# Attention and a cosine-gated feed-forward on one core: work moved from VectorE to Pool, a new order in a step, and split copies

## The chip, the cores and the metric

The kernel runs on one core of a Trainium2 chip. A core has a matmul engine (TensorE, PE in the profile), a vector engine (VectorE, DVE), a scalar engine (ScalarE, ACT), a general engine (Pool, POOL) and a queue engine that issues transfers (SyncE, SP). They run side by side and wait for each other by semaphores. Each works through its own instructions in the order in which the program gives them. The metric is the device time of one execution in microseconds (us); lower is better. All times below are from chip runs of the kernel before the change.

## The reference

Eight batches of 512 tokens, eight heads of 64 columns and 32 state rows per head. Tokens read the state and the state reads the tokens (two softmax attentions). The 544 rows of a batch, 512 columns wide, then pass through a feed-forward layer with 2048 hidden columns whose gate is h cos h:

```python
scores = scale * x @ state.T;  a = softmax(scores);   xread = a @ state
scores2 = scale * state @ x.T; a2 = softmax(scores2); sread = a2 @ x
y = concat([xread, sread], axis=2)        # (8, 8, 544, 64)
x = y.transpose(0, 2, 1, 3).reshape(4352, 512)
h = x @ w_in                               # (4352, 2048)
out = (h * cos(h)) @ w_out                 # (4352, 512)
```

x and state are float32. w_in and w_out arrive as float64 and are used as float32.

## The kernel before

**Main loop.** One step of the loop at L746 works one tile of 128 hidden columns. Steps 0 to 127 are the token tiles: batch b = step // 16, tile f = step % 16, 512 tokens wide. Steps 128 to 143 are the state tiles, all 256 state rows at once; their n-th tile has f = (n + 8) % 16. A step makes h (`hidden`, L416) in one of two PSUM buffers, then the gate: ScalarE adds a large constant to round (`gate`, L425), VectorE takes the remainder (`gate2`, L428), ScalarE takes Abs and Sin (`gate3`, L433 and L434), VectorE multiplies by h (`gate4`, L440). The result g goes to one of 28 slots of g_all. The products with w_out (`output`, L555) come three steps later (`LAG`).

**Attention inside h.** h is not made from the attention's output. For each batch the product of the state with w_in is made first (`products`, L389) and copied to the tile sw (`products_kept`, L394); h is sw times the softmax weights aT. The products of batches 0 and 1 use the PSUM banks o1* (SIDE), those of later batches the banks at*.

**The order in a step.** It is written out by hand at L753 to L798. `plan(b)` (L666) gives lists for each step: attention work for TensorE (`go(0)`), for ScalarE after `gate` (`go(1)`) and after `gate3` (`go(2)`), for VectorE after `gate2` (`go(3)`) and after the product (`go(4)`). In `plan`, `early` is the scores and softmax of a batch (tokens are transposed twice, then scores, maximum, spread, exponentials, sums, normalisation) and `late` is the reading of the tokens by the state (two transposes `turn`, two matmul groups `reads`, the scaling `keep`, the transpose `turned`). The last reads of a batch release the loads of the next batch's x on SP's queue.

**Pairs of batches.** Two batches form a pair, and their four half-batches of g (phase 0 to 3, eight tiles each) are multiplied with the quarters of w_out (a11, a12, a21, a22) by a scheme with seven products in place of eight. It needs sums of weight quarters (s1 to s4, `blocks`, L731: eight instructions of 128x1024 at steps 13 to 23) and differences of g (`minus`, L442, called from `sums` and `sums2`: one per step in phase 2, three in phase 3). Two of the products run in the next pair's steps (`more`). When the first product of phase 0 or 2 is complete, `keep_product` (L491) copies both channels of its PSUM bank (MAIN) to a held tile, and only then may TensorE start the next product in that bank.

**Conversion.** A float64 weight becomes float32 in parts (`convert_part`, L198): "1" Abs of the high words and "2" the low words on ScalarE, "a" a maximum, "b" a shift, "c" an xor and "d" a 32-bit integer addition of e on VectorE. Eighteen loads are converted, four of them ahead of the loop and one in each of steps 0 to 13; part d of a load runs in the step after its other parts. s3 overwrites the quarter a21; two more loads (L161) bring it back, and they are converted at steps 136 and 137, with part d one step later. The state tiles need the quarter again from step 139 on.

Of the kernel before, what the change touches and what calls it, by code (L numbers as in the profile page):

```python
# [23 lines left out]
def kernel(  # L24
# [164 lines left out]
    def convert(i, parts):  # L189


        if i < len(loads) and f64:
            for p in parts:
                convert_part(i, p)
        if "c" in parts and i + 3 < N_LOADS:
            fetch(i + 4)

    def convert_part(i, p):  # L198
# [15 lines left out]
        elif p == "c":  # L214
            nc.vector.scalar_tensor_tensor(out=bits, in0=raw[:, :, :, 1],
                                           scalar=-2 ** 31, in1=bits,
                                           op0=ALU.bitwise_and,
                                           op1=ALU.bitwise_xor)
        else:
            nc.vector.tensor_tensor(bits, bits, e.bitcast(I32), op=ALU.add)  # L220
# [6 lines left out]
    class Attention:  # L227
# [166 lines left out]
        def products_kept(self, nt, bank=None, c0=0, c1=WC):  # L394
# [47 lines left out]
    def minus(out, a, b):  # L442
        nc.vector.tensor_tensor(out, a, b, op=ALU.subtract)  # L443
# [47 lines left out]
    def keep_product(out, bank):  # L491
        for ch in range(2):
            nc.scalar.activation(out.t[:, ch], acc[bank][ch], func=ACTF.Copy,  # L493
                                 scale=TWO_PI)
# [26 lines left out]
    def sums(t):  # L521
        pr, i = t.pair, t.i
        pr.b[t.phase, i] = t
        if t.phase == 2:
            minus(pr.b[0, i].g, t.g, pr.b[0, i].g)
        if t.phase == 3:
            minus(pr.b[0, i].g, t.g, pr.b[0, i].g)
            minus(pr.b[2, i].g, t.g, pr.b[2, i].g)

    def sums2(t):  # L530
        pr, i = t.pair, t.i
        if t.phase == 3:
            minus(pr.b[1, i].g, pr.b[1, i].g, pr.b[0, i].g)
# [132 lines left out]
    def plan(b):  # L666
# [38 lines left out]
        if b == 0:  # L705
# [23 lines left out]
    conv_at.update({B * NF + 8: N_LOADS, B * NF + 9: N_LOADS + 1})  # L729

    def blocks(op, out_, a, b, r):  # L731
        nc.vector.tensor_tensor(out_[:, r], a[:, r], b[:, r], op=op)
# [13 lines left out]
    for step, t in enumerate(tiles()):  # L746
# [27 lines left out]
        if last >= 0:  # L774
            convert(last, "d")
# [14 lines left out]
        if conv >= 0:  # L790
            convert(conv, "bc")
# [39 lines left out]
```

## Time and profile before

| | |
|---|---|
| time, median of 3 runs | 855.65 us (855.56 to 857.0) |
| the profiled execution's own time | 852.41 us |
| its span, first to last instruction | 850.6 us |
| mean granted TensorE clock | 0.972 |
| busy: TensorE, VectorE, ScalarE, Pool | 776.4, 481.1, 405.1, 3.1 us |
| chain of work that ended last | TensorE 73%, VectorE 13%, ScalarE 10% |

The profile is of one execution. A row of a group view gives line, engine, operation, the tiles written and read, shapes and count, then the busy time and the mean of one in ns, then the idle time of the engine just before them and what ended it. A row in order of time gives start, length, engine, line, operation, tiles and count; in brackets is the idle time of the engine before it and what ended that. A row of waits names the waiting engine and line, the one waited for, the total in us, how often, and the longest. A row of stretches gives the length, the busy time and the count of instructions of each engine, the granted clock, the share of the DMA engines and GB/s. Each fp32 matmul shows as two matmul instructions.

### The profile page before, as it was taken

The page shows a single profiled execution, that of the slowest core. Times are in us where ns is not written, and L with a number is a line of the kernel's source. Part 1 is how long each engine was busy: PE and PEld are TensorE (multiplying, and loading weights), DVE is VectorE, ACT ScalarE, POOL GpSimd, SP SyncE. Part 2 cuts the span into 40 slices and gives each one's busy share as a digit, 9 for nine tenths or more (in the row PEclk, how much of TensorE's full clock was granted, in tenths as well). Part 3 has the DMA queues.
Part 4 walks back from the last instruction along what each step waited for, and adds up shares of the span by engine and source line. Part 5 has one row for each costly group of instructions (what it writes and reads, how often), then busy time and mean ns, then how long its engine had stood idle before and what let it go on. Part 6 is the DMA issues. An engine that isn't in the chain of part 4 may idle for free.

```text
span 850.6 us, 7375 instructions
## 1 busy us (share of the span) xinstructions
PE 776.4 (91%) x2720; PEld 347.6 (41%) x2720; DVE 481.1 (57%) x757; ACT 405.1 (48%) x666; POOL 3.1 (0%) x10
## 2 busy tenths in 40 slices
PE   2578688979999999989999999899999999999997
PEld 1223233333444443444444344344444444455444
DVE  3878986876437345676354446763563456642431
ACT  2667684454436444633446444634464544321312
POOL 1000000000000000000000000000000000000000
PEclk9789889999999999999999999999999999999999
DMA  6584412102001202030010211030010110301021
GB/s 148 188 233 149 148 50 50 25 0 50 0 1 26 49 13 37 1 64 11 1 25 3 48 27 25 11 63 0 7 19 1 26 25 12 113 1 17 8 38 37
DMA packets 110499, 37.17 MB, mean 44 GB/s; under 512 B 102464, under 2 KB 102464, under 8 KB 110464
## 3 DMA queue, kind: packets, MB, share of 16 engines
q1 hardware_dynamic: 109248, 36.19, 18.4%
q10 hardware_dynamic: 1088, 0.26, 0.2%
q8 instruction: 21, 0.34, 0.2%
q0 software_dynamic: 128, 0.26, 0.2%
q14 instruction: 14, 0.11, 0.0%
HBM read 27.79 MB, written 8.91 MB: 43 GB/s over the span
## 4 chain that ended last, share of the span: by engine, by line
PE 73%; DVE 13%; ACT 10%; issue 1%; DMA 1%; SPq 0%; DVEq 0%
PE o L481 38%; PE h L419 24%; PE at L274 4%; PE o L593 3%; DVE q L428 2%; ACT q L434 2%; ACT q L433 2%; DVE g_all L443 2%; PE at L361 1%; ACT q L425 1%; DVE g_all L440 1%; PE at L247 1%; DVE xT L294 1%; DMA x_b<-in_x_dram 1%; DVE w_out L220 1%
## 5 line engine op out<-in xcount | busy, mean ns | idle before, releaser
L419 PE MATMUL h<-aT,sw 128*128 128x512 f32 x512 | 251.8, 615 | 7.2 <-DVE g_all L440 6.7
L481 PE MATMUL o<-g_all,w_out 128*128 128x512 f32 x512 | 238.6, 602 | 11.9 <-ACT held L493 7.7
L425 ACT ACTIVATE q<-h 128x512 f32<-128x512 f32 (+1 forms) x144 | 82.2, 571 | 299.5 <-PE h L419 299.5
L428 DVE SCALAR_TENSOR_TENSOR q<-q,h 128x512 f32<-128x512 f32 (+1 forms) x144 | 94.3, 655 | 207.9 <-ACT q L425 207.7
L481 PE MATMUL o<-g_all,s 128*128 128x512 f32 x384 | 178.6, 602 | 7.9 <-ACT held L493 7.5
L440 DVE TENSOR_TENSOR g_all<-h,q 128x512 f32<-128x512 f32 (+1 forms) x144 | 94.9, 659 | 122.9 <-ACT q L434 122.7
L481 PEld LDWEIGHTS o<-g_all,w_out 128*128 128x128 f32 x512 | 99.0, 194 | 138.5 <-issue 120.6
L419 PEld LDWEIGHTS h<-aT,sw 128*128 128x128 f32 x512 | 92.1, 193 | 128.1 <-issue 93.2
L433 ACT ACTIVATE q<-q 128x512 f32<-128x512 f32 (+1 forms) x144 | 87.9, 611 | 108.5 <-DVE q L428 108.5
L481 PEld LDWEIGHTS o<-g_all,s 128*128 128x128 f32 x384 | 73.5, 193 | 102.5 <-issue 85.3
L434 ACT ACTIVATE q<-q,halfpi 128x512 f32<-128x512 f32 (+1 forms) x144 | 100.5, 698 | 4.5
L443 DVE TENSOR_TENSOR g_all<-g_all 128x512 f32<-128x512 f32 x128 | 82.9, 687 | 2.3
L593 PE MATMUL o<-w_out,g_all 128*128 128x512 f32 x64 | 31.0, 615 | 4.1 <-DVE w_out L220 4.1
L419 PE MATMUL h<-sT,w_in 128*128 128x256 f32 x128 | 30.2, 379 | 0.0
L487 DVE SCALAR_TENSOR_TENSOR held<-o,held 128x512 f32<-128x512 f32 x40 | 25.4, 681 | 7.8 <-PE o L481 7.8
L419 PEld LDWEIGHTS h<-sT,w_in 128*128 128x128 f32 x128 | 24.3, 190 | 10.1 <-issue 6.7
L274 PE MATMUL at<-w_in,stT 64*32 64x512 f32 x384 | 26.1, 601 | 0.0
L399 ACT COPY sw<-at 128x512 f32<-128x512 f32 x48 | 25.6, 590 | 0.0
L274 PE MATMUL o<-w_in,stT 64*32 64x512 f32 (+1 forms) x144 | 12.2, 585 | 12.0 <-DVE w_in L220 12.0
L507 DVE STREAM_TRANSPOSE ot<-held 128x512 f32<-128x512 f32 x32 | 22.3, 697 | 0.0
L361 PE MATMUL at<-x_b,xT 128*64 128x128 f32 x256 | 17.5, 279 | 4.8 <-ACT xT L349 4.8
L247 PE MATMUL at<-ident,x_b 128*128 128x128 f32 x112 | 15.4, 275 | 6.3 <-ACT xT L256 6.3
(75 smaller groups left out, 403.2 us busy)
## 6 DMA issues: line engine op xcount, KB each, us to landing
out_dram<-ot SPq DMA_DIRECT2D x136, 64.0 KB, 2.0
x_b<-in_x_dram SPq DMA_DIRECT2D x32, 256.0 KB, 4.6
g_all<-in_moe_w_out_dram SPq DMA_DIRECT2D x8, 1024.0 KB, 5.0
g_all<-in_moe_w_in_dram SPq DMA_DIRECT2D x6, 1024.0 KB, 5.2
g_all<-in_moe_w_in_dram SPq DMA_DIRECT2D x4, 512.0 KB, 7.4
x_b<-in_moe_w_out_dram SPq DMA_DIRECT2D x1, 1024.0 KB, 5.6
xT<-in_moe_w_out_dram SPq DMA_DIRECT2D x1, 1024.0 KB, 7.7
s<-in_state_dram ACTq DMA_DIRECT2D x4, 64.0 KB, 5.4
```

What stands on the lines that cost most here:

```text
L274: nc.tensor.matmul(out=(to or at)[j][Ns * k:Ns * k + Ns, 0:n], lhsT=w[D * j:D * j + D, self.b, Ns * k:Ns * k + Ns], rhs=r(slice(D * j, D * ...
L361: nc.tensor.matmul(out=at[0][rows, cols], lhsT=self.a2T[:, j, c, rows], rhs=x_c[:, j, k:k + 2], start=(c == 0), stop=(c == NC - 1), tile_p ...
L399: nc.scalar.copy(sw_of[self.b, nt][:, j, c0:c1], to[j][:, 0:c1 - c0])
L419: nc.tensor.matmul(out=t.hp, lhsT=t.lhs(i), rhs=t.rhs(i), start=(i == 0), stop=(i == t.kn - 1))
L425: nc.scalar.activation(t.q, t.hp, func=ACTF.Copy, bias=MAGIC)
L428: nc.vector.scalar_tensor_tensor(out=t.q, in0=t.q, scalar=MAGIC, in1=t.hp, op0=ALU.subtract, op1=ALU.subtract)
L433: nc.scalar.activation(t.q, t.q, func=ACTF.Abs)
L434: nc.scalar.activation(t.q, t.q, func=ACTF.Sin, bias=halfpi, scale=-TWO_PI)
L440: nc.vector.tensor_tensor(t.g, t.hp, t.q, op=ALU.mult)
L443: nc.vector.tensor_tensor(out, a, b, op=ALU.subtract)
L481: nc.tensor.matmul(out=acc[bank][ch], lhsT=w[:, i, P * ch:P * ch + P], rhs=g.g, start=(i == 0), stop=(i == NH - 1))
L593: nc.tensor.matmul(out=acc[MAIN][i], lhsT=t.g[:, P * i:P * i + P], rhs=w_out[:, :, t.f, :], start=(n == 0), stop=(n == NF - 1))
```

## The change

- Part d of the conversion runs on Pool for loads 4 and up, in the same step as the parts before it, after part c. Loads 0 to 3 keep it on VectorE.
- `blocks`, the sums of weight quarters, runs on Pool.
- `minus` runs on Pool for the first pair and stays on VectorE for the other three.
- `products_kept` of batches 0 and 1 moves to VectorE (after `gate2`), but for the very first piece.
- `keep_product` copies channel 0 on ScalarE as before and channel 1 on VectorE.
- In every step `hidden` comes ahead of `go(0)`; before, that was so in step 1 alone.
- In `plan(0)`, `turned` of batch 0 moves from step 5 to 4, and `early` and `late` of batch 1 one step forward.
- The two reloads are converted at steps 133 and 135.

```diff
         else:
-            nc.vector.tensor_tensor(bits, bits, e.bitcast(I32), op=ALU.add)
+            engine = nc.vector if i < 4 else nc.gpsimd
+            engine.tensor_tensor(bits, bits, e.bitcast(I32), op=ALU.add)
...
-                nc.scalar.copy(sw_of[self.b, nt][:, j, c0:c1],
-                               to[j][:, 0:c1 - c0])
+                dst = sw_of[self.b, nt][:, j, c0:c1]
+                if self.b < 2 and (nt, c0) != (0, 0):
+                    nc.vector.tensor_copy(dst, to[j][:, 0:c1 - c0])
+                else:
+                    nc.scalar.copy(dst, to[j][:, 0:c1 - c0])
...
-    def minus(out, a, b):
-        nc.vector.tensor_tensor(out, a, b, op=ALU.subtract)
+    def minus(pr, out, a, b):
+        engine = nc.gpsimd if pr.n == 0 else nc.vector
+        engine.tensor_tensor(out, a, b, op=ALU.subtract)
...
     def keep_product(out, bank):
-        for ch in range(2):
-            nc.scalar.activation(out.t[:, ch], acc[bank][ch], func=ACTF.Copy,
-                                 scale=TWO_PI)
+        nc.scalar.activation(out.t[:, 0], acc[bank][0], func=ACTF.Copy,
+                             scale=TWO_PI)
+        nc.vector.tensor_scalar(out.t[:, 1], acc[bank][1], TWO_PI, None,
+                                op0=ALU.mult)
...
-            x_act[s].append((b, "products_kept", nt) + bank)
+            to = x_dve if b < 2 else x_act
+            to[s].append((b, "products_kept", nt) + bank)
...
-            late(0, (1, 2, 3, 5))
-            early(1, (6, 7, 8, 9, 10, 11, 12))
-            late(1, (13, 14, 15))
+            late(0, (1, 2, 3, 4))
+            early(1, (5, 6, 7, 8, 9, 10, 11))
+            late(1, (12, 13, 14))
...
-    conv_at.update({B * NF + 8: N_LOADS, B * NF + 9: N_LOADS + 1})
+    conv_at.update({B * NF + 5: N_LOADS, B * NF + 7: N_LOADS + 1})
 
     def blocks(op, out_, a, b, r):
-        nc.vector.tensor_tensor(out_[:, r], a[:, r], b[:, r], op=op)
+        nc.gpsimd.tensor_tensor(out_[:, r], a[:, r], b[:, r], op=op)
...
-        last, conv = conv_at.get(step - 1, -1), conv_at.get(step, -1)
-        if step == 0:
-            last = 3
+        conv = conv_at.get(step, -1)
...
-        if step != 1:
-            go(0)
+        hidden(t)
+        go(0)
         if step == 4:
             states(1, acc[SIDE][1])
-        hidden(t)
-        if step == 1:
-            go(0)
...
-        if last >= 0:
-            convert(last, "d")
+        if step == 0:
+            convert(3, "d")
...
         if conv >= 0:
-            convert(conv, "bc")
+            convert(conv, "bcd")
```

More of the change, by code (lines that the diff above doesn't have):

```diff
@@ L524, in sums @@
         if t.phase == 2:
-            minus(pr.b[0, i].g, t.g, pr.b[0, i].g)
+            minus(pr, pr.b[0, i].g, t.g, pr.b[0, i].g)
         if t.phase == 3:
-            minus(pr.b[0, i].g, t.g, pr.b[0, i].g)
-            minus(pr.b[2, i].g, t.g, pr.b[2, i].g)
+            minus(pr, pr.b[0, i].g, t.g, pr.b[0, i].g)
+            minus(pr, pr.b[2, i].g, t.g, pr.b[2, i].g)
     def sums2(t):
@@ L532, in sums2 @@
         if t.phase == 3:
-            minus(pr.b[1, i].g, pr.b[1, i].g, pr.b[0, i].g)
+            minus(pr, pr.b[1, i].g, pr.b[1, i].g, pr.b[0, i].g)
     def free(t):
```

## The prediction

> **What bounds the kernel now.** I read the share of each engine first, then five stretches of the span cut at starts of the first gate instruction (ScalarE's L425, one per step of the main loop), then the list of waits, then the instructions in order of time at the places that the list names.
>
> The stretches are: preparation; steps 0 to 13; steps 14 to 26; steps 27 to 127; the state steps.
>
> ```profile
> core 0: us, PE busy (x) PEld busy (x) DVE busy (x) ACT busy (x) POOL busy (x), PEclk, DMA share, GB/s
> 0.00:33.25 33.25, 13.00 (x60) 6.52 (x60) 18.81 (x33) 9.97 (x19) 3.15 (x10) 0.79 0.63 164
> 33.25:126.99 93.74, 68.55 (x282) 28.40 (x281) 77.00 (x105) 70.41 (x102) 0.00 (x0) 0.87 0.47 150
> 126.99:194.51 67.52, 56.63 (x223) 24.28 (x223) 51.14 (x76) 36.28 (x62) 0.00 (x0) 0.97 0.14 24
> 194.51:745.80 551.29, 543.14 (x1879) 235.16 (x1878) 300.47 (x485) 262.35 (x435) 0.00 (x0) 1.00 0.14 25
> 745.80:850.60 104.80, 95.09 (x281) 53.27 (x279) 33.66 (x62) 26.07 (x54) 0.00 (x0) 0.98 0.12 20
> sum 850.60, PE 776.42 PEld 347.63 DVE 481.08 ACT 405.08 POOL 3.15; mean PE 155.28 PEld 69.53 DVE 96.22 ACT 81.02 POOL 0.63
> ```
>
> TensorE is busy for 776.4 of 850.6 us, so at most 74.2 us can be won of its idle time, beside what a reduced clock costs. By stretch the idle time (length minus PE busy) is 20.3, 25.2, 10.9, 8.2 and 9.7 us. The first is the preparation, in which the diff changes nothing. In steps 0 to 13 no engine is full: VectorE works 77.0 of 93.74 us, ScalarE 70.4, TensorE 68.6 at a granted clock of 0.87. There the engines hand work to each other in a chain. From step 27 on TensorE is the bound (543.14 of 551.29). The waits:
>
> ```profile
> PE o L481 <- ACT held L493: 15.2, 5, 7.7
> PE at L247 <- ACT xT L256: 6.3, 4, 2.3
> PE h L419 <- DVE g_all L440: 6.7, 3, 3.0
> PE at L378 <- DVE sr L372: 2.4, 1, 2.4
> PE o L481 <- DVE w_out L220: 4.2, 1, 4.2
> ```
>
> **Steps 0 to 13: the integer additions go to Pool.** VectorE's loop at its densest, and the prices:
>
> ```profile
> 99.92 1.22 DVE L215 SCALAR_TENSOR_TENSOR w_out<-g_all,w_out 128x1024 int32<-128x1024 int32 x1
> 101.06 0.68 DVE L428 SCALAR_TENSOR_TENSOR q<-q,h 128x512 f32<-128x512 f32 x1
> 101.66 1.22 DVE L220 CUSTOM_DVE_ANT_0 w_out<-w_out,s 128x2048 uint16<-128x2048 uint16 x1
> 102.80 0.68 DVE L210 TENSOR_SCALAR w_out<-w_out 128x1024 f32<-128x1024 f32 x1
> ...
> L220 DVE CUSTOM_DVE_ANT_0 w_out<-w_out,s 128x2048 uint16<-128x2048 uint16 x10 | 12.1, 1208 | 0.0
> L732 DVE TENSOR_TENSOR s<-w_out,s 128x1024 f32<-128x1024 f32 x2 | 2.4, 1219 | 0.0
> L267 DVE COPY xT<-o 128x512 f32<-128x512 f32 x2 | 1.4, 691 | 12.3 <-PE o L247 12.3
> masks.py:199 POOL TENSOR_SCALAR_AFFINE_SELECT ident<-ident 128x128 f32<-128x128 f32 x1 | 0.3, 289 | 0.1
> ```
>
> Of the additions (L220, 1.2 us), 13 lie in this stretch and leave VectorE: -15.6. One weight sum (L732, 1.2) leaves: -1.2. In return VectorE takes the product copies of steps 1 (two half-width ones, 0.4 each by the width), 3, 7, 11 and 13 (two each, at 0.69 by the row of L267, the same copy out of the same memory), and one held channel: 0.8 + 5.5 + 0.7 = +7.0. Net -9.8, from 77.0 to 67.2 us. If VectorE keeps its share of 82%, the stretch falls from 93.7 to 81.8: a gain of 12, the upper end. ScalarE loses the same copies, so it does not become the bound; TensorE's 68.6 leaves room, too.
>
> No row shows Pool adding two tensors. From below it takes what VectorE takes, 1.2 us for 1024 columns. Pool's only elementwise row, the select with one operand, takes 289 ns for 128 columns, 2.3 us for 1024; twice that for two operands, 4.6, is the end from above. I take 2.3 for 1024 and 1.2 for 512 columns, since the row of the same engine counts the start of an instruction eight times over. That hides in a step (93.74/14 = 6.7 us) if nothing else waits for Pool. What can wait is the next conversion on VectorE. The addition now starts when the xor (L215) ends, at 101.14 in the rows above, and before, the next maximum (L210) started at 102.80, 1.66 us on. If Pool's addition keeps VectorE's conversion instructions from starting, the maximum comes at 2.3, 0.65 later per step; if not, it comes 1.14 (the spacing 101.66 to 102.80) earlier. Held off, about half of the 14 steps have attention work or copies between the two that fill the hole, so the loss is 7 x 0.65 = 4.6: the lower end is -5.
>
> The Trainium skill speaks against this part: "SBUF — State Buffer", section "Who interferes with whom", says that a VectorE instruction with two SBUF inputs, or in a two-port mode, and a Pool instruction that reads SBUF exclude each other for the whole instruction. The rows here fit the precondition, since the 1024-column shift and maximum (0.68 us) run at twice the pace of the xor (1.22); no Pool row here overlaps them, so the lock itself is not shown. By that rule the stretch would gain about nothing, without it about 12.
>
> The new order helps in both cases. h of step 3 no longer stands behind products that wait for the conversion, and the 4.2 us wait of L481 for w_out shrinks, since the addition starts right after the xor rather than behind the next step's attention work. The two-token wait (2.3, the longest of L247's four) goes. I take +7 for the stretch, between -5 and +12.
>
> **Steps 14 to 26: 10.9 us idle.**
>
> ```profile
> 149.32 0.66 PE L247 MATMUL at<-ident,x_b 128*128 128x128 f32 x4 [1.75 <-ACT xT L256]
> 175.87 1.98 PE L419 MATMUL h<-aT,sw 128*128 128x512 f32 x4 [1.08 <-DVE g_all L440]
> 183.49 2.57 PE L419 MATMUL h<-aT,sw 128*128 128x512 f32 x4 [3.04 <-DVE g_all L440]
> ```
>
> The attention of the second batch moves up one step, with its x loads on SP's queue; the reads that release them come one step earlier, so the loads do. The wait of L378 (2.4) for the state rows goes: they are made two steps ahead. One of L247's waits (1.75, at 149.32) goes, as h fills the hole. Six weight sums (7.2 us) and 17 differences (8 + 3 x 3, 0.63 us each by the row at 371.89 below) leave VectorE for Pool, and three pairs of copies come: about 13 us less in a stretch with 51 us of VectorE. Of the three waits of h for the gate (6.7 together), two lie here: the one of 1.08 is VectorE's backlog and goes; of the one of 3.04 I count 1, since it hangs on ScalarE's exponentials and table loads, untouched. The held wait here (of the 15.2 of five, 7.7 lie in the first stretch and 5.9 in the next part, which leaves 1.6) shortens by 1.2: the pair's differences no longer stand ahead of the second channel. Sum 2.4 + 1.75 + 1.1 + 1 + 1.2 = 7.5, at most 10.9, at least 4. Pool, whose queue issues DMAs only at the very start, carries at most three differences (3.6 us) or one sum and one difference (3.5) per step against 5.2 us per step, and the first reader of a difference comes three steps later, so no one waits for it. Without that cover, each microsecond beyond the step is TensorE's.
>
> **Steps 27 to 127: two small gains, three losses.** The 8.2 us idle are two token waits and three held waits (two of 2.58, one of 0.70):
>
> ```profile
> 319.64 0.57 ACT L256 COPY xT<-at 128x512 f32<-128x512 f32 x1
> 320.26 0.66 PE L247 MATMUL at<-ident,x_b 128*128 128x128 f32 x4 [1.15 <-ACT xT L256]
> ...
> 371.51 1.09 ACT L493 ACTIVATE held<-o 128x512 f32<-128x512 f32 x2
> 371.89 1.90 DVE L443 TENSOR_TENSOR g_all<-g_all 128x512 f32<-128x512 f32 x3
> 372.16 2.64 PE L481 MATMUL o<-g_all,s 128*128 128x512 f32 x3 [2.58 <-ACT held L493]
> ...
> 720.87 1.07 ACT L493 ACTIVATE held<-o 128x512 f32<-128x512 f32 x2
> 721.72 1.89 DVE L443 TENSOR_TENSOR g_all<-g_all 128x512 f32<-128x512 f32 x3
> 721.50 3.27 PE L481 MATMUL o<-g_all,s 128*128 128x512 f32 x7 [0.70 <-ACT held L493]
> ```
>
> With h ahead of the tokens, TensorE has 1.7 us of work at 319.1 while ScalarE finishes at 320.2: 2 x 1.15 = 2.3 won.
>
> The split of the held copies costs here. It is emitted after the step's differences, and in the later pairs these stay on VectorE. Channel 0 is ready as before (371.51 + 0.6). Channel 1 was ready at 372.60; now it stands behind the gate and three differences, which end at 373.79, and takes 0.69: 374.48. TensorE does channel 0's two passes from 372.16 to 373.02 and waits 1.43. The same rows come again one pair later, and at 721.50 it waits from 722.36 to 723.61 + 0.69 = 724.3, 1.94. Together -4.8. The chain before it (exponentials, differences) is ScalarE's and VectorE's own, so an earlier h does not pull it forward. Behind the late copy stands the next step's second gate instruction, 0.7 later; the h that needs its buffer is two steps off. The other held copies (first half of a pair) have no differences ahead and no wait: nothing, with a bound of one copy, 0.7, either way.
>
> **The state steps.** The reload of the overwritten quarter is converted at steps 133 and 135 rather than 136 and 137:
>
> ```profile
> 726.91 0.45 SPq L178 DMA_DIRECT2D x_b<-in_moe_w_out_dram  x1
> 797.23 1.88 PE L593 MATMUL o<-w_out,g_all 128*128 128x512 f32 x4
> 797.43 0.39 ACT L425 ACTIVATE q<-h 128x256 f32<-128x256 f32 x1 [5.05 <-PE h L419]
> 801.13 1.23 DVE L215 SCALAR_TENSOR_TENSOR w_out<-x_b,w_out 128x1024 int32<-128x1024 int32 x1
> 804.31 0.38 ACT L425 ACTIVATE q<-h 128x256 f32<-128x256 f32 x1 [3.57 <-PE h L419]
> 805.06 1.22 DVE L220 CUSTOM_DVE_ANT_0 w_out<-w_out,s 128x2048 uint16<-128x2048 uint16 x1
> 806.33 1.98 PE L593 MATMUL o<-w_out,g_all 128*128 128x512 f32 x4 [2.06 <-DVE w_out L220]
> 815.54 3.15 PE L593 MATMUL o<-w_out,g_all 128*128 128x512 f32 x4 [2.06 <-DVE w_out L220]
> 824.42 0.39 ACT L425 ACTIVATE q<-h 128x256 f32<-128x256 f32 x1 [9.07 <-PE h L419]
> ```
>
> A step takes 6.88 us (797.43 to 804.31); the next two take 20.11, 6.35 over, of which 4.1 is waiting for L220 and the rest slower matmuls after it. The outputs at 806.33 read other columns than L220 writes, and yet start 0.05 us after it. The output at 797.23 comes in program order behind the xor of 801.13 and did not wait for it. So the wait hangs on the form of VectorE's integer addition, a custom instruction on uint16, and a plain Pool addition should not have it; the columns themselves are needed six steps later. The loads are issued 50 us ahead (726.91 against 3 x 6.88 before 797.7). I take +6.35, between +4 and +6.4.
>
> **Sum.** 7 + 7.5 + 2.3 - 4.8 + 6.35 = 18.35. The profiled execution took 852.41 us (its span and 1.8), so 834.1; the median shown is 3.2 above that execution, so 837.
>
> **Rivals.**
> (a) Pool's additions hold VectorE off, as above. For it: the maximum follows the xor within 1.66 us, less than 2.3. Against it: VectorE idles 16.7 us in that stretch, which hides some. The first stretch gives 0: 844.
> (b) Nothing is held off and the new order frees the chain wholly: first stretch 14, second 10, the rest as above: 27.9, 828. Against it: the exponentials' 3.0 us wait stays.
> (c) The false wait stays with the Pool addition. It now stands in the same step ahead of the outputs of steps 133 and 135: from the gate through the xor 4.9 us (797.43 to 802.36), then 2.3 on Pool, 7.2 twice against 4.1 now. That turns +6.35 into -10: 854. Against it: 797.23.
> (d) Slower: Pool takes 4.6 us for 1024 columns and holds VectorE's conversions. A step of the first stretch then needs 4.6 + 3.3 (maximum and shift at 0.68, gate 0.69, xor 1.22) = 7.9, 14 of them 110 rather than 93.7: -16 in place of +7. Three differences take 6.9 per step where 5.5 were needed (551.29/101): -11 over eight steps, and the second stretch's gain goes: 18.35 - 23 - 11 - 7.5 = -23, 879. Each microsecond of Pool costs 14, so it decides from 2.3 + 18.35/14 = 3.6 us per addition.
>
> **How the numbers follow.** Forecast 45%, (a) 21%, (b) 16%, (c) 8%, (d) 10%. Under 0.2% (1.7 us) nothing can be told from no change. (c) is on that line, so half of it counts as same: faster 0.86, same 0.04, slower 0.10. The range takes in (a), (b) and the ends of the terms, and stops short of (c) and (d): 825 to 853.
>
> **What would show it.** Right: no L593 wait for a conversion; no L247 wait after step 32; three longer L481 waits, now released by VectorE's held copy, at the second-half starts of the last three pairs; Pool additions near 2.3 us; steps 0 to 13 near 87 us, 14 to 26 near 60. Wrong: Pool rows of 3.6 us or more, maximum rows that start only when Pool's addition ends and a first stretch no shorter than 93 us, or an L593 wait for Pool at steps 133 and 135.

## The result and the profile after

The change brings 855.65 us to **834.97 us** (median of 4 runs, 832.4 to 835.97; the kernel before beside it 856.33, 855.56 to 857.99). The ratio is 0.9743, with a 95% interval of 0.9716 to 0.9771: 21 us or 2.6% faster. The forecast was 837.0 us. The profiled execution took 835.97 us, span 834.2, against 852.41 and 850.6 before. In that pair the difference is 16.4 us; the rest to 21 lies in the scatter of the single executions, 3.6 us for the changed kernel alone.

The changed kernel from step 0 on, in four stretches cut like those of before (length, then busy time of TensorE, its weight load, VectorE, ScalarE and Pool, then the granted clock); the last cut is the first gate instruction of step 128, which before is at 747.57:

```profile
33.10:121.45 88.35, 66.76 (x281) 28.29 (x281) 78.83 (x100) 66.74 (x92) 30.69 (x13) 0.86 0.50 158
121.45:180.17 58.72, 55.07 (x225) 24.05 (x225) 39.20 (x60) 33.51 (x55) 37.54 (x23) 1.00 0.15 27
180.17:737.47 557.30, 549.07 (x1891) 238.73 (x1888) 296.53 (x477) 261.79 (x430) 23.30 (x19) 0.99 0.13 25
737.47:834.18 96.71, 91.09 (x272) 51.30 (x270) 29.89 (x57) 26.12 (x54) 4.70 (x2) 0.98 0.13 22
```

Steps 0 to 13 fell from 93.74 to 88.35 us, steps 14 to 26 from 67.52 to 58.72, the state steps from 103.0 (850.6 - 747.57) to 96.7. Steps 27 to 127 grew, from 553.1 (747.57 - 194.51; the prediction cut them 1.8 us too early, at 745.80) to 557.3. The gains less this loss, 5.4 + 8.8 + 6.3 - 4.2, with 0.1 of the preparation, make the 16.4. Pool is now busy for 30.7 of 88.35 us in the first stretch and 37.5 of 58.7 in the second.

What TensorE waits for now, from the list of waits (total, times, longest, in us):

```profile
PE o L490 <- ACT held L501: 11.4, 3, 5.8
PE h L425 <- DVE g_all L446: 9.4, 5, 3.0
PE h L425 <- DVE sw L404: 5.4, 2, 4.1
PE o L490 <- POOL w_out L223: 3.4, 1, 3.4
PE o L490 <- DVE held L503: 3.2, 4, 1.6
```

The waits for tokens (xT), for the state rows (sr) and, in the state steps, for a converted weight are no longer in the list. Three are new: h waits for product copies (sw) that VectorE now makes, one output waits for Pool's addition, and four outputs wait for the held channel that VectorE now copies.

Pool's new work, by groups (tiles, shapes and count; busy us, mean ns of one):

```profile
L452 POOL TENSOR_TENSOR g_all<-g_all 128x512 f32<-128x512 f32 x32 | 40.0, 1276 | 26.2 <-DVE g_all L446 17.7 <-issue 4.0 <-PE at L250 3.6
L223 POOL TENSOR_TENSOR w_out<-w_out,s 128x1024 int32<-128x1024 int32 x10 | 23.6, 2359 | 603.9 <-DVE w_out L217 599.5 <-ACT s L209 4.4
L743 POOL TENSOR_TENSOR s<-w_out,s 128x1024 f32<-128x1024 f32 x2 | 4.7, 2366 | 0.0
```

An addition of 1024 columns takes 2.36 us, of integers as of floats, and a difference of 512 takes 1.28.

### The profile page after: what moved, and what is told of

It reads as the page before. It is cut to its first block, busy times and chain, and to the rows that moved or that the text cites. A ratio compares the mean times of both kernels' runs of the same rounds, so it can differ in the third digit from the quotient of the medians.

```text
span 834.2 us, 7432 instructions
## 1 busy us (share of the span) xinstructions
PE 775.2 (93%) x2720; PEld 349.1 (42%) x2720; DVE 463.3 (56%) x723; ACT 398.1 (48%) x644; POOL 99.4 (12%) x66
## 4 chain that ended last, share of the span: by engine, by line
PE 76%; DVE 13%; ACT 7%; issue 1%; DMA 1%; POOL 0%; SPq 0%; DVEq 0%; POOLq 0%
PE o L490 41%; PE h L425 25%; PE at L277 4%; PE o L603 3%; DVE q L434 2%; ACT q L440 1%; DVE g_all L452 1%; DVE w_out L212 1%; PE at L250 1%; ACT q L439 1%; PE at L364 1%; DVE g_all L446 1%; DVE xT L297 1%; DMA x_b<-in_x_dram 1%; DVE w_out L217 1%
## 5 line engine op out<-in xcount | busy, mean ns | idle before, releaser
L425 PE MATMUL h<-aT,sw 128*128 128x512 f32 x512 | 247.0, 606 | 15.3 <-DVE g_all L446 9.4
L434 DVE SCALAR_TENSOR_TENSOR q<-q,h 128x512 f32<-128x512 f32 (+1 forms) x144 | 94.4, 656 | 201.7 <-ACT q L431 201.6
L490 PE MATMUL o<-g_all,s 128*128 128x512 f32 x384 | 184.4, 616 | 8.2 <-ACT held L501 5.6
L425 PEld LDWEIGHTS h<-aT,sw 128*128 128x128 f32 x512 | 98.9, 195 | 144.1 <-issue 115.5
L490 PEld LDWEIGHTS o<-g_all,w_out 128*128 128x128 f32 x512 | 94.7, 192 | 131.5 <-issue 122.3
L439 ACT ACTIVATE q<-q 128x512 f32<-128x512 f32 (+1 forms) x144 | 87.7, 609 | 103.2 <-DVE q L434 103.1
L490 PEld LDWEIGHTS o<-g_all,s 128*128 128x128 f32 x384 | 71.4, 195 | 102.9 <-issue 84.5
L223 POOL TENSOR_TENSOR w_out<-w_out,s 128x1024 int32<-128x1024 int32 x10 | 23.6, 2359 | 603.9 <-DVE w_out L217 599.5
L452 DVE TENSOR_TENSOR g_all<-g_all 128x512 f32<-128x512 f32 x96 | 62.2, 688 | 1.6
L452 POOL TENSOR_TENSOR g_all<-g_all 128x512 f32<-128x512 f32 x32 | 40.0, 1276 | 26.2 <-DVE g_all L446 17.7
L425 PEld LDWEIGHTS h<-sT,w_in 128*128 128x128 f32 x128 | 24.3, 190 | 10.1 <-issue 6.7
L496 DVE SCALAR_TENSOR_TENSOR held<-o,held 128x512 f32<-128x512 f32 x40 | 25.5, 682 | 4.3 <-PE o L490 4.3
L223 POOL TENSOR_TENSOR w_in<-w_in,s 128x1024 int32<-128x1024 int32 x6 | 14.2, 2361 | 57.6 <-DVE w_in L217 57.6
```

Source lines behind the costliest of these rows:

```text
L223: engine.tensor_tensor(bits, bits, e.bitcast(I32), op=ALU.add)
L425: nc.tensor.matmul(out=t.hp, lhsT=t.lhs(i), rhs=t.rhs(i), start=(i == 0), stop=(i == t.kn - 1))
L434: nc.vector.scalar_tensor_tensor(out=t.q, in0=t.q, scalar=MAGIC, in1=t.hp, op0=ALU.subtract, op1=ALU.subtract)
L439: nc.scalar.activation(t.q, t.q, func=ACTF.Abs)
L452: engine.tensor_tensor(out, a, b, op=ALU.subtract)
L490: nc.tensor.matmul(out=acc[bank][ch], lhsT=w[:, i, P * ch:P * ch + P], rhs=g.g, start=(i == 0), stop=(i == NH - 1))
```

## The experiments

The kernel before has medians from 852.64 to 856.33 us on the chips used, so medians are compared only between kernels run beside each other, and ratios go by the runs of before that stood beside. This table has the length of each stretch in the profile of each kernel, in us, cut at the first gate instructions of steps 0, 14, 27, 46, 78, 110 and 128 (differences of starts; the last column before the median is the span's end less the start of step 128):

| kernel | 0-13 | 14-26 | 27-45 | 46-77 | 78-109 | 110-127 | state | median |
|---|---|---|---|---|---|---|---|---|
| before | 93.7 | 67.5 | 106.4 | 179.7 | 178.0 | 89.0 | 103.0 | 856.33 |
| after | 88.4 | 58.7 | 105.7 | 179.8 | 180.4 | 91.4 | 96.7 | 834.97 |
| after, again | 88.3 | 58.7 | 105.7 | 179.8 | 180.4 | 91.4 | 96.7 | 835.47 |
| before, h first | 87.7 | 64.9 | 105.2 | 178.1 | 179.5 | 89.5 | 101.4 | 843.48 |
| after, attention first | 92.5 | 59.9 | 106.7 | 181.1 | 181.0 | 91.0 | 96.7 | 842.8 |
| additions on VectorE | 101.6 | 62.1 | 105.7 | 180.1 | 180.5 | 91.4 | 96.7 | 852.05 |
| product copies on ScalarE | 86.3 | 57.7 | 105.7 | 178.0 | 179.5 | 89.5 | 96.7 | 829.33 |
| both of these | 99.9 | 59.8 | 105.7 | 178.1 | 179.5 | 89.5 | 96.7 | 843.19 |
| later maximum | 87.8 | 58.7 | 105.7 | 179.6 | 178.6 | 93.1 | 96.7 | 834.51 |
| Pool adds twice | 96.4 | 61.6 | 105.7 | 179.5 | 178.5 | 93.1 | 96.7 | 847.9 |
| differences on VectorE | 88.2 | 67.6 | 107.1 | 179.8 | 180.4 | 91.4 | 97.1 | 846.54 |
| held copies on ScalarE | 88.0 | 59.4 | 105.2 | 179.5 | 178.1 | 89.5 | 96.7 | 830.98 |
| before, early reload | 93.5 | 67.5 | 106.4 | 179.7 | 178.0 | 89.0 | 103.1 | 855.03 |
| after, late reload | 87.0 | 58.0 | 105.7 | 180.5 | 180.7 | 91.4 | 96.7 | 834.6 |

**The changed kernel once more**, as the mark for the runs beside it.

> The changed kernel as it is, beside the next two on the same chip. 0.974 of the kernel before, so 832 to 836.

It took 835.47 us; the ratio to the kernel before is 0.9758 (0.9733 to 0.9783). The stretches of these two profiles agree to 0.1 us from step 0 on. But the last kernel of the table, which is the changed one up to step 132, has 87.0 and 58.0 in the first two and 452.6 for 451.6 us in steps 46 to 127. So a stretch is known to about 1.4, 0.7 and 1.0 us there, and less than that isn't read as a difference below.

**The order alone, in the kernel before.**

```diff
-        if step != 1:
-            go(0)
+        hidden(t)
+        go(0)
         if step == 4:
             states(1, acc[SIDE][1])
-        hidden(t)
-        if step == 1:
-            go(0)
```

> The kernel before with one edit: h ahead of the attention work on TensorE in every step. Theory: the four token waits of TensorE (6.4 us in all) go, of which the two in steps 49 and 81 (2.3) and the one of step 18 (1.75) are won in full, and in steps 0 to 13 one or two more: 850 to 852. Rival: in the first 27 steps VectorE and ScalarE set the pace, so only the 2.3 us of steps 49 and 81 are won: 853.5 to 855.

843.48 us against 854.42, ratio 0.9877 (0.9856 to 0.9898): **10.9 us from the order alone**, half of the whole gain and more than was expected. Steps 0 to 13 fall to 87.7, as low as in the changed kernel (87.0 to 88.4). The stretch of this kernel (columns as above):

```profile
32.80:120.53 87.73, 67.56 (x283) 28.20 (x283) 76.61 (x105) 70.07 (x101) 0.00 (x0) 0.90 0.51 160
```

VectorE is busy for 76.6 us in it, as before the change (77.0), Pool for none. TensorE idles 20.2 us in it for 25.2 before, and is busy 1.0 less. So the stretch got 6.0 us shorter without one instruction leaving VectorE.

**The order undone, in the changed kernel**: the same lines the other way round in the changed kernel.

> The changed kernel with the attention work ahead of h again in every step but step 1. Theory: if h first is worth here what it was worth alone in the kernel before (6.0 us in steps 0 to 13, 2.6 in 14 to 26, 2.3 at the token waits, 10.9 in all), 844 to 847. Rival: the other parts of the change remove the same waits, so that it is worth only the 2.3 us of the later token waits and 1 to 2 more: 837 to 839.

842.8 us, ratio 0.9854 (0.983 to 0.9878), 7.3 more than the changed kernel beside it. This lies between the two expectations: the order is worth less here than the 10.9 alone. The waits that come back:

```profile
PE at L250 <- ACT xT L259: 5.3, 4, 1.8
PE o L277 <- POOL w_in L223: 4.1, 1, 4.1
PE at L381 <- DVE sr L375: 3.1, 2, 2.3
PE at L364 <- ACT xT L352: 2.7, 2, 2.6
```

They are 15.2 us, and none of them is in the changed kernel's list. They are waits of attention and product matmuls for an input. When h stands ahead of them, TensorE has 1.7 us of work that is ready while the input is made. Some of that is given back: with h first, h waits 9.4 us for gates and 5.4 for product copies; here it waits 5.1 and 0.7.

**The integer additions back on VectorE** for the loads of steps 0 to 13, in the place that they have in the changed kernel, right after the xor of the same step.

```diff
-            engine = nc.vector if i < 4 else nc.gpsimd
+            engine = nc.vector if i < N_LOADS else nc.gpsimd
```

> The changed kernel with the integer additions of steps 0 to 13 on VectorE again (those of the two reloads stay on Pool), in the place that they have in the changed kernel. VectorE gets 14 x 1.2 = 17 us back, and the stretched maximum rows (12 us over their 0.69) go. Theory: the hold takes back most of what moving them won, so the first stretch changes by less than 3 us: 833 to 838. Rival: the move is worth what leaves VectorE, 12 us at its share of the stretch: 845 to 849. Second rival: the hold costs more than it wins, 830 to 832.

852.05 us, ratio 0.9962 (0.9944 to 0.998): 17.5 more than the changed kernel with the late reload (834.6, run beside it). The first stretch takes 101.6 us, 13.2 more. That is above all three expectations. Was it VectorE's time, with the product copies there too? The next two runs ask that.

**Product copies on ScalarE again**, and the held channel split only in the first pair's second half; the additions stay on Pool.

```diff
-            to = x_dve if b < 2 else x_act
+            to = x_act
...
-                if self.b < 2 and (nt, c0) != (0, 0):
-                    nc.vector.tensor_copy(dst, to[j][:, 0:c1 - c0])
-                else:
-                    nc.scalar.copy(dst, to[j][:, 0:c1 - c0])
+                nc.scalar.copy(dst, to[j][:, 0:c1 - c0])
...
-    def keep_product(out, bank):
+    def keep_product(out, bank, split=False):
...
+        if split:
+            nc.vector.tensor_scalar(out.t[:, 1], acc[bank][1], TWO_PI, None,
+                                    op0=ALU.mult)
+        else:
+            nc.scalar.activation(out.t[:, 1], acc[bank][1], func=ACTF.Copy,
+                                 scale=TWO_PI)
...
+            keep_product(pr.p5, MAIN, pr.n == 0)
```

> The changed kernel with the product copies of batches 0 and 1 on ScalarE again, and the held copy split at the first pair's phase 2 alone. VectorE loses 6 us of copies in steps 0 to 13, and 3.6 in steps 14 to 26. Theory: h first is what shortened steps 0 to 13 (87.7 us with it alone, 88.4 with the whole change), and the copies on VectorE took back what the additions gave; without them the stretch falls to 83 to 86 us, steps 14 to 26 stay near 58, and the later pairs get the 3 to 5 us that the run with both channels on ScalarE showed: 826 to 830 in all. Rival: ScalarE sets the pace of steps 0 to 13, and 6 us of copies there make the stretch longer, 90 to 93 us: 832 to 836 in all.

**829.33 us**, ratio 0.9689 (0.9663 to 0.9715): 6.1 less than the changed kernel beside it, and the fastest kernel of this study. The first stretch is 86.3, 0.7 to 2.1 below the changed kernel's. With a scatter of 1.4 this suggests, and doesn't show, that the copies' move cost something there. In the changed kernel h waits 4.1 us for a copy that VectorE makes behind a gate. The row of the list for this kernel:

```profile
PE h L422 <- ACT sw L403: 2.8, 2, 2.4
```

The larger part of the 6 us is the held channel: steps 46 to 127 take 447.0 for 451.6 us.

**Both**: the kernel just shown, with the additions of steps 0 to 13 on VectorE.

> The kernel with the product copies back on ScalarE, and in addition the integer additions of steps 0 to 13 back on VectorE (those of the two reloads stay on Pool). With the copies on VectorE the same move of the additions cost 13.2 us in steps 0 to 13 (88.4 to 101.6). Theory 1, the additions on Pool only make room for the copies, which did not need to be on VectorE: the stretch stays near the 87.7 that the kernel before with only h moved forward has, so 86 to 90 (86.3 with the additions on Pool), and the whole comes out at 829 to 834 us. Theory 2, the additions cost VectorE's chain their time wherever the copies are: 14 times 1.2 = 17 us less what idle time swallows, the stretch is 96 to 100 and the whole 839 to 844 us.

843.19 us, ratio 0.9879 (0.9858 to 0.99); first stretch 99.9, 13.6 over the 86.3. The number is that of the second theory, and the first one falls: the additions on VectorE cost the same wherever the copies are. But the reason given for that number, VectorE's time, isn't what the trace shows. This kernel, in order of time:

```profile
34.47 0.62 PE L277 MATMUL o<-w_in,stT 64*32 64x256 f32 x4
40.89 1.23 DVE L223 CUSTOM_DVE_ANT_0 w_in<-w_in,s 128x2048 uint16<-128x2048 uint16 x1
42.17 1.09 PE L277 MATMUL o<-w_in,stT 64*32 64x256 f32 x12 [7.08 <-DVE w_in L223]
83.47 1.01 PE L277 MATMUL o<-w_in,stT 64*32 64x512 f32 x6 [4.96 <-DVE w_in L223]
```

And the kernel with Pool's additions:

```profile
35.35 0.64 PE L277 MATMUL o<-w_in,stT 64*32 64x256 f32 x8
36.29 0.64 PE L277 MATMUL o<-w_in,stT 64*32 64x256 f32 x8 [0.30 <-DVE w_in L223]
39.86 1.23 DVE L217 SCALAR_TENSOR_TENSOR w_in<-g_all,w_in 128x1024 int32<-128x1024 int32 x1
41.24 2.36 POOL L223 TENSOR_TENSOR w_in<-w_in,s 128x1024 int32<-128x1024 int32 x1 [37.27 <-DVE w_in L217]
```

With Pool's addition the sixteen products of that step are done at 36.93, before the load's xor has begun at 39.86: they read other columns. With VectorE's addition twelve of the sixteen wait for it, 7.08 us, and start 0.05 us after its end. The products at 83.47 stand behind another of these additions for 4.96; with Pool's, no product waits at that step. These two waits are 12.0 us, but that is not a net sum: with Pool's additions h waits 2.4 for a product copy and eight products 1.3 for Pool, and here neither does. All of TensorE's idle time in the stretch is 28.1 here for 18.0 there, 10.1 of the 13.6 us, and the rest is that TensorE is busy 3.5 longer. The first of the two is the false wait of the state steps, on w_in in place of w_out. In the kernel before, the addition came one step later, behind the step's products in program order: with h first and the additions there, the stretch is 87.7. Pool's part is thus that it permits the addition in the same step. Against the old place, the whole of what the two kernels differ by in this stretch (the additions, a weight sum, a held channel, the earlier attention steps) is worth 87.7 - 86.3 = 1.4 us, which is no more than a stretch scatters, and not 13. No run moves the additions alone, so it isn't shown that they gain nothing; another part may have taken back what they gave.

**The maximum out of the way**: part a after `gate4` rather than ahead of it, so that it no longer runs against the addition of the step before.

```diff
-        if conv >= 0:
-            convert(conv, "a")
         gate3(t)
...
         gate4(t)
+        if conv >= 0:
+            convert(conv, "a")
```

> The changed kernel with one edit: the maximum of a conversion (part a) comes on VectorE after the gate's product rather than ahead of it. Nothing is left out. Theory: Pool's addition holds the maximum off (its rows stretch from 0.69 to as much as 2.55 us and end after the Pool row ends) and the product behind it is late by as much; later in the step the Pool row has ended, so the maximum rows go back to 0.69 and steps 0 to 13 shorten by 3 to 6 us: 829 to 832. Rival: those rows are long but the step waits for ScalarE anyway: rows of 0.69 and no gain, 834 to 836. A second rival: the hold moves to the shift or the xor behind it, and these rows stretch.

First, what the changed kernel shows in order of time:

```profile
65.66 0.68 DVE L434 SCALAR_TENSOR_TENSOR q<-q,h 128x512 f32<-128x512 f32 x1
65.89 2.37 POOL L223 TENSOR_TENSOR w_in<-w_in,s 128x1024 int32<-128x1024 int32 x1 [5.14 <-DVE w_in L217]
66.27 2.54 DVE L212 TENSOR_SCALAR w_out<-w_out 128x1024 f32<-128x1024 f32 x1
72.00 2.37 POOL L223 TENSOR_TENSOR w_out<-w_out,s 128x1024 int32<-128x1024 int32 x1 [3.75 <-DVE w_out L217]
72.38 2.55 DVE L212 TENSOR_SCALAR w_in<-w_in 128x1024 f32<-128x1024 f32 x1
```

The maximum (L212), 0.68 us before the change, takes 2.54, and ends 0.55 us after Pool's row both times (68.81 after 68.26; 74.93 after 74.37). The gate (L434), with one input in PSUM, keeps its 0.68. **The hold-off is real**; 8 of the 14 maxima of these steps are stretched, and the mean of the ten on w_out is 1598 ns. The Trainium skill, "SBUF — State Buffer", section "Who interferes with whom", says that a VectorE instruction in a two-port mode, which one of the maximum's kind (`tensor_scalar`) can enter, and a Pool instruction block each other, and that one with at most one SBUF input and outside the two-port modes doesn't contend. The trace agrees: the maximum is held (2.54 us), the gate isn't (0.68).

With the later maximum the group of these rows is back at its own length:

```profile
L212 DVE TENSOR_SCALAR w_out<-w_out 128x1024 f32<-128x1024 f32 x10 | 6.8, 683 | 0.0
```

And its stretch of steps 0 to 13 has 68.0 us of VectorE's work:

```profile
32.95:120.74 87.79, 64.73 (x282) 27.43 (x283) 67.95 (x100) 66.67 (x92) 30.70 (x13) 0.90 0.50 160
```

The time is 834.51 us, ratio 0.9778 (0.9758 to 0.9799): the change's own time, and with 87.8 us a stretch inside its scatter. So freeing VectorE of 10.9 us (78.8 - 68.0) of holding in this way is worth nothing that can be told, as the rival had it. Either these lay in time in which the step waited for something else, or the later place of the maximum cost what they gave; no run separates the two.

**Pool's additions doubled**: behind each of the 14 additions a second one of the same size, into a tile that nothing reads. (It computes more than the reference asks, and leaves nothing out.)

```diff
             engine.tensor_tensor(bits, bits, e.bitcast(I32), op=ALU.add)
+            if 4 <= i < N_LOADS:
...
+                nc.gpsimd.tensor_tensor(spare, e, e, op=ALU.add)
```

> The changed kernel with a second addition on Pool behind each integer addition of steps 0 to 13 (same size, its result is not used). It doubles Pool's time and adds nothing to VectorE, ScalarE or TensorE. Theory: as Pool's row holds off VectorE's conversion instructions, each of the 14 steps grows by up to 2.4 us less what the step has to spare: steps 0 to 13 longer by 12 to 30 us, 847 to 865, with maximum, shift or xor rows stretched by more than now. Rival: Pool delays only what reads its results; these have over two steps to spare, and doubling costs 0 to 4 us: 835 to 839, and the rows do not stretch further.

847.9 us, ratio 0.9934 (0.9914 to 0.9953): 13.4 more than the run above beside it. The time is at the low end of the theory's; steps 0 to 13, 8.0 longer than in the changed kernel's profile, stay under its 12, and steps 14 to 26 are 2.9 longer. So the price sets in somewhere between 2.4 and 4.6 us of Pool's time per step. The groups of the maximum and the shift:

```profile
L212 DVE TENSOR_SCALAR w_out<-w_out 128x1024 f32<-128x1024 f32 x10 | 18.5, 1848 | 1.2 <-ACT w_out L206 1.2
L214 DVE TENSOR_SCALAR w_out<-w_out 128x1024 int32<-128x1024 int32 x10 | 11.6, 1165 | 0.0
```

Now the shift, behind the maximum, is held as well (1165 ns for 688). What stands behind it on VectorE comes later: the xor (1226 ns) and the gate (685) keep their lengths. Not all of the price need be this: an output, too, waits longer for Pool's addition itself (4.5 us for 3.4 in the changed kernel).

**The first pair's differences on VectorE**, with the rest of the change.

```diff
-        engine = nc.gpsimd if pr.n == 0 else nc.vector
+        engine = nc.vector
```

> The changed kernel with the first pair's differences on VectorE again (32 instructions of 0.63 us; 17 of them in steps 14 to 26). Theory: VectorE is near its limit in those steps, and at step 26 the held copy's channel 1 then stands behind three differences as in the later pairs: 1.4 us there and 1 to 3 us of waits of h for the gate come back: 837.5 to 840. Rival: steps 14 to 26 have room by now: 835 to 836.

846.54 us, ratio 0.9913 (0.9898 to 0.9927), 11.9 more than the 834.6 beside it and above both expectations. Steps 14 to 26 take 67.6 us, as before the change, and steps 27 to 45 1.4 more. Steps 14 to 26 as a stretch:

```profile
121.53:189.14 67.61, 59.18 (x225) 25.64 (x225) 51.39 (x74) 33.36 (x55) 21.80 (x9) 0.95 0.13 24
```

One of the differences, and the two longest waits of TensorE, in order of time:

```profile
144.06 2.31 DVE L452 TENSOR_TENSOR g_all<-g_all 128x512 f32<-128x512 f32 x1
147.12 2.80 PE L490 MATMUL o<-g_all,s 128*128 128x512 f32 x4 [2.64 <-DVE held L496]
177.81 2.83 PE L425 MATMUL h<-aT,sw 128*128 128x512 f32 x4 [2.69 <-DVE g_all L446]
```

VectorE has 51.4 us of work rather than 39.2. TensorE idles 8.4 rather than 3.7, with a wait of 2.64 for a sum that VectorE makes late (held, L496) and 2.69 for a gate, and its clock is 0.95 rather than 1.00. The waits of the changed kernel in the same steps:

```profile
128.59 1.98 PE L425 MATMUL h<-aT,sw 128*128 128x512 f32 x4 [0.80 <-DVE g_all L446]
171.78 1.98 PE L425 MATMUL h<-aT,sw 128*128 128x512 f32 x4 [1.87 <-DVE g_all L446]
177.35 1.98 PE L425 MATMUL h<-aT,sw 128*128 128x512 f32 x4 [0.98 <-DVE g_all L446]
```

So the place of the differences is worth 8.9 us here, more than the whole gain of the stretch in the forecast. But not all of it is load. Three of these differences take 2.00 to 2.32 us for 0.69: they run beside Pool's weight sums, and the one shown ends 0.55 us after such a sum (143.47 to 145.82), as the maxima do. The held sum (L496) that TensorE waits for at 147.12 stands behind it. With sums and differences all on VectorE, in the old kernel with h first, the stretch is 64.9 and not 67.6.

**The held channels both on ScalarE**, with the rest of the change.

```diff
-        nc.scalar.activation(out.t[:, 0], acc[bank][0], func=ACTF.Copy,
-                             scale=TWO_PI)
-        nc.vector.tensor_scalar(out.t[:, 1], acc[bank][1], TWO_PI, None,
-                                op0=ALU.mult)
+        for ch in range(2):
+            nc.scalar.activation(out.t[:, ch], acc[bank][ch], func=ACTF.Copy,
+                                 scale=TWO_PI)
```

> The changed kernel with both channels of every held copy on ScalarE again. My theory: the split costs at the second-half starts of the last three pairs, where channel 1 stands behind three differences on VectorE; by the prediction 1.43 + 1.43 + 1.94 = 4.8 us, and up to 7 with the slower matmuls after the longer waits, against under 1 us that it gains at the first pair. So 829 to 831 us, against 835.0 for the changed kernel, and the L490 waits for VectorE's held copy gone. Rival: the split is neutral, since channel 0's matmuls cover channel 1's wait (0.2 and 0.6 us of waiting are left in two of the three places): 835, within 1 us.

830.98 us, ratio 0.9733 (0.971 to 0.9756), 3.5 less than the later maximum beside it; its interval overlaps that of the changed kernel's own ratio, so the stretches have to decide. The time is the one expected for a split that costs. Steps 46 to 127 take 447.1 us against 451.6: the split costs 4.5, give or take 1. Step 58 of the changed kernel, and the end of step 122:

```profile
356.59 1.90 DVE L452 TENSOR_TENSOR g_all<-g_all 128x512 f32<-128x512 f32 x3
356.85 2.08 PE L490 MATMUL o<-g_all,s 128*128 128x512 f32 x2 [2.79 <-ACT held L501]
358.40 0.68 DVE L503 TENSOR_SCALAR held<-o 128x512 f32<-128x512 f32 x1
359.14 4.78 PE L490 MATMUL o<-g_all,s 128*128 128x512 f32 x6 [0.21 <-DVE held L503]
...
711.52 0.68 DVE L503 TENSOR_SCALAR held<-o 128x512 f32<-128x512 f32 x1
712.26 2.84 PE L490 MATMUL o<-g_all,s 128*128 128x512 f32 x6 [1.65 <-DVE held L503]
```

Channel 1 stands behind three differences and is ready at 359.08. TensorE waits for it only 0.21 us, since the two passes of channel 0, 0.43 us each elsewhere, took 2.08 together. Granted clock around the place (the number behind the busy times):

```profile
354.00:357.00 3.00, 0.21 (x3) 0.15 (x1) 2.14 (x4) 2.52 (x5) 0.00 (x0) 0.87 0.28 44
357.00:360.00 3.00, 2.79 (x3) 0.85 (x4) 3.00 (x6) 0.58 (x2) 0.00 (x0) 0.50 0.28 44
360.00:363.00 3.00, 3.00 (x5) 1.29 (x4) 2.14 (x4) 1.07 (x2) 0.00 (x0) 0.50 0.46 73
363.00:366.00 3.00, 3.00 (x14) 1.25 (x15) 0.76 (x2) 0.33 (x1) 0.00 (x0) 0.99 0.10 15
```

The clock falls to 0.50 after the 2.79 us in which TensorE waits for channel 0, and comes back some 6 us later. The delay of channel 1 thus shows here mostly as slow matmuls and not as a wait. Without the split, the kernel with h first in the old program has the same wait, and then:

```profile
361.54 5.37 PE L481 MATMUL o<-g_all,s 128*128 128x512 f32 x8 [2.78 <-ACT held L493]
539.65 6.75 PE L481 MATMUL o<-g_all,s 128*128 128x512 f32 x8 [2.78 <-ACT held L493]
```

The kernel before had these eight passes in 5.40 (at 372.16) and 3.70 us (at 551.83). After one and the same wait, 2.58 to 2.78 us, eight equal passes took 3.70, 5.37 or 6.75 us.

**The reload's new steps alone**, in the kernel before, and **the old steps** in the changed kernel.

```diff
-    conv_at.update({B * NF + 8: N_LOADS, B * NF + 9: N_LOADS + 1})
+    conv_at.update({B * NF + 5: N_LOADS, B * NF + 7: N_LOADS + 1})
```

> The kernel before with one edit: the two reloads are converted at steps 133 and 135 rather than 136 and 137; the additions stay on VectorE, one step after the other parts. My theory, as in the prediction: the wait of the state outputs hangs on the form of VectorE's integer addition and not on when it comes, so two L593 waits of about 2 us stay, only earlier: 855 to 857 as before. Rival: the earlier time alone takes the wait away: 6.35 us less, 849 to 851, and no L593 wait.

> The changed kernel with the two reloads converted at steps 136 and 137 as before, with their additions on Pool. Theory: a plain Pool addition is not waited for by outputs that read other columns, so the later time costs nothing while the columns come before step 139: 834 to 836, no L603 wait. Rival: the time is what took the wait away: 2 to 6 us more, 837 to 841.

Before with early reload: 855.03 us, ratio 1.0019 (0.9999 to 1.0038), no gain, and its list of waits has the same line:

```profile
PE o L593 <- DVE w_out L220: 4.1, 2, 2.1
```

Changed with late reload: 834.6 us, ratio 0.9772 (0.9755 to 0.9789), and a state stretch of 96.7 us as in the changed kernel. Pool's addition for the first of the two reloads and the outputs beside it:

```profile
791.39 2.35 POOL L223 TENSOR_TENSOR w_out<-w_out,s 128x1024 int32<-128x1024 int32 x1 [582.38 <-DVE w_out L217]
792.96 1.88 PE L603 MATMUL o<-w_out,g_all 128*128 128x512 f32 x4
```

The outputs start at 792.96, while Pool adds until 793.74. In the kernel before they start when VectorE's addition has ended. The gain of the state steps is that of the engine that adds, and the steps chosen for it are worth nothing.

## Why the prediction was right, and where it wasn't

The sum, 18.35, lies between the difference of the profiled pair (16.4) and that of the medians (21.4), and the time came out 2.0 us from the median. That is better than the working deserves: two of its terms had the right size for the wrong reason, and there the match is luck. The forecast of faster rests on firmer ground, since the order alone gives 10.9 us and the state steps 6.3.

**Steps 0 to 13: +7 forecast, +5.3 measured.** VectorE's load was worked out right: 67.2 us were forecast, and 68.0 remain once the maxima aren't held. The step that failed is the price by load, "if VectorE keeps its share of 82%, the stretch falls from 93.7 to 81.8": with 76.6 us on VectorE and h first, the stretch is 87.7; with 68.0 and the whole change, 87.8. The order, which I let "help in both cases" without a number, is worth 6.0 alone. Additions and copies together come to nothing that a stretch can tell: 1.4 between the best kernel and the order alone, and 0.7 to 2.1 that go with the copies and a held channel, all of it near the scatter. I had counted these copies as load and named no one who waits for them, though h does (5.4 us for VectorE's copies, 2.8 for ScalarE's). The output's wait for w_out fell from 4.2 only to 3.4. That Pool is slower isn't the reason: with the addition on VectorE in the same step the wait is 3.9.

**The hold-off** of rival (a) exists just as its rule has it, but its price was not seen: taking it off the maxima changed nothing beyond the scatter, where the forecast put 4.6 as the lower end's loss and the rival a whole gain of 7. Pool's 2.36 and 1.28 us were forecast at 2.3 and 1.2. With two additions per step, 4.6 us, the first stretch loses 8.0, where rival (d) had 23 (from +7 to -16) for additions of that length. Its sum of 7.9 us per step let nothing of the step overlap Pool's row, and the gate, which isn't held, did.

**Steps 14 to 26: +7.5 forecast, +8.8 measured.** Of the terms, the waits for sr (2.4) and tokens (1.75) went; h first alone gives 2.6 here. The gate's waits went from 1.08 + 3.04 to 0.80 + 1.87 + 0.98, so the 2.1 credited there came to 0.5. What is left of the 8.8, about 6.2, goes with the sums and differences that leave VectorE, the product copies that it takes and the earlier attention, which no run separates; the 8.9 us of taking the differences back can't be added to the rest, as the hold-off is in it. In the forecast the differences stood behind one held wait (1.2) and one backlog (1.1), and that term was too small. TensorE's idle time fell by 7.2 of the 8.8 us; the rest is that its passes are faster, at a clock of 1.00 for 0.97, a term that the forecast didn't have.

**Steps 27 to 127: -2.5 forecast, -4.2 measured.** The two token waits gave 2.7 (steps 49 and 81 take 4.31 us for 5.67), forecast 2.3, and the start of the stretch 0.7. The split costs 4.5, forecast 4.8, but only 2.5 of it as waits (0.21, 0.64 and 1.65, where 1.43, 1.43 and 1.94 were forecast) and the rest as slow matmuls. The term that was missing is the clock after the wait for channel 0: with h first, the second of these places takes 6.75 in place of 3.70 us, 3.0 lost, and that takes back the token waits. The two kernels with all these copies on ScalarE in the changed program have 6.73 and 5.40, and 5.28 and 6.71, so one place of each kind, too. What decides after which wait the clock is slow, and for how long, was not tried and stays open.

**State steps: +6.35 forecast, +6.3 measured**, by the mechanism given. (Of the 6.35, 4.1 were the waits and 2.2 slow passes after them; in the old program with h first the same waits cost 2.33 each, 4.7, so this part of the term is not fixed.) No output waits for a conversion, and the runs on the reload and on the additions show that it is VectorE's integer addition, not the timing, that makes the wait. Rival (c) falls. I saw it only where the list of waits had it; that the same false wait would have struck the first step's products, had the additions moved forward on VectorE, was not in the forecast.

Rival (b) at 828 is near what the best kernel reaches (829.33), but it gets there by other means: by the copies and the held channel going back to ScalarE.

## What to carry to other kernels

Cost a move between engines by who waits for the result and not by the share of busy time: 10.9 us came from letting a matmul that was ready go first, while steps 0 to 13 took 87.7 us with 76.6 us of work on VectorE and 87.8 with 68.0. When a wait's release follows within 0.05 us of an instruction that doesn't make the data waited for, look at the form of that instruction, since an engine with a plainer form may remove the wait although it is twice as slow. A copy that frees a bank belongs on the engine that gets to it first: take its place in the queue from the trace before splitting it.

## What was not expected of the hardware

- A tiny instruction is held, too, until Pool's row has ended. The two rows of the changed kernel:

```profile
51.06 2.36 POOL L223 TENSOR_TENSOR w_out<-w_out,s 128x1024 int32<-128x1024 int32 x1 [3.16 <-DVE w_out L217]
52.63 0.82 DVE L333 TENSOR_SCALAR i<-i 128x2 f32<-128x2 f32 x1
```

The 128x2 scaling takes 0.16 us in the kernel with all additions of these steps on VectorE, and here ends at 53.45, 0.03 us after Pool.
- Pool's time for 1024 columns is the same for integers (2359 ns) and floats (2366), and twice VectorE's 1.2 us.
- The clock after a wait of 2.8 us can fall to 0.50 for about 6 us, so such a wait costs up to twice its length. A shorter one can do it as well: after the wait of 1.65 us that ends at 712.26 in the changed kernel, eight passes took 3.70 us, and after the same wait in the kernels with the later maximum and with two additions on Pool 5.40. That is the 93.1 for 91.4 of these two in the table.
